# Two column blocks resized to 376, the first block in units of four chunks, the second by banks with the turns between the next step's matmuls

## The chip, the core and the metric

The kernel runs on one core of a Trainium2 chip. Its engines work side by side and meet through semaphores: PE multiplies matrices into PSUM, ACT and DVE read PSUM and write SBUF, POOL issues the loads of the input and computes a little, SP issues the stores of the output. The metric is the device time of one execution in microseconds; lower is better.

## What is computed

The input `x` is 8 x 3008 x 256. A Fourier transform over the sequence and over the width is taken, of it the real part, and each of its 24064 rows goes through a feed-forward layer of 2048 hidden units with a squared relu:

```python
X = np.fft.fft(np.fft.fft(x, axis=1), axis=2).real      # 8 x 3008 x 256
h = np.maximum(X.reshape(24064, 256) @ w_in, 0.0)       # 24064 x 2048
out = (h * h) @ w_out                                    # 24064 x 256
```

## The kernel before

**The columns.** The transform along the sequence is made from tables of sines and cosines and from folded input, so that a *unit* (batch, even or odd frequencies) gives PE matmuls with results in a PSUM tile `pz` (`z_steps`, matmuls at L565). Of each unit one half of the columns is copied from PSUM by ACT (L576, or L583 where it was put off), the other half is made by DVE as twice an earlier partial sum `es` less the result (L594). They land in two SBUF rows of columns, `zc` (cosine part) and `zs` (sine part). All columns stand in one sequence, units one behind the other: unit (0,0) holds columns 0 to 751, unit (1,0) 752 to 1503, its first 376 copied and its last 376 made by DVE, unit (0,1) begins at 1504. The sequence is cut into *blocks* (`wins`): the first few by `FIRST` (L58), the rest of 512.

**A block.** For a block of `wn` columns the hidden layer has 16 *chunks* of 128 units; a *step* `s` takes two chunks. `gh` holds the transformed first weight in three rows of blocks: cosine, sine, and -2 times sine (the *turn*). A step is: `pq(s)`, four matmuls into a PSUM tile `ph` of two banks, one chunk to a bank (cosine L793, sine L794); `relu(s, 0)`, by ACT into `h2` columns 0 to `wn`; `turn(s)`, two matmuls (L816) that add the turn row to the same PSUM tile, which makes of each column the hidden values of the mirrored frequency; `relu(s, 1)`, by ACT, reversed, into columns `wn` to 2 `wn`; and later `power(s)`, DVE's square of `h2` (L833). The PSUM pool for `ph` has two tiles (`ps_h`, `bufs=2`), as have `ps_o` and `ps_z`.

**What lies between.** The order is written out by hand, engine by engine. Behind `pq(s)` and `relu(s, 0)` stands `others(s)`: the step's share of the *second product* of the block before (`ffn2_steps`: groups of 128 output rows, two jobs of eight matmuls a group at L678, a copy of the result by ACT at L693 and stores by SP), folds of the next batch's input on DVE, table steps, and, from step `lo` on, the z matmuls of the units that the next block needs. A block of `wn` columns gives the next block 2 `wn`/128 groups, rounded up: eight groups (16 jobs of eight) for 512, four (8 jobs) for 240.

**Block 0** (240 columns) is taken two steps at a time: two `pq`, two relus, the others, two turns, two relus. Its `others` make the later parts of `gh`: `gh_step(cc)` is four matmuls for 512 hidden units (L511), and `gh_scale` brings them to SBUF, by DVE (L501) or ACT (L499); `gh_turn` makes the turn row (L518). `gh_step(1)` is called ahead of the block, into one tile of `ps_h`, and scaled by one DVE operation. `z0(0,2)` and `z0(1,2)` are the copies and the DVE half of the columns that block 0 left over. `gh_nyq` (16 small matmuls, L526, and a DVE copy) makes `g2n`, which is first read in block 4.

**Block 1** (512 columns) has one job of the second product in a step, and its first relu is two ACT operations, one to a bank (L825). Its `others` fold batch 1: the fold ends in `od`, which `nyq` (L438, `py`) and the z matmuls of steps 6 and 7 read. Block 4 takes in its steps 4 and 6 another way, in which DVE does the second relu (`cosines` L802, `twice` L806, `sines` L811, L827).

Of the kernel before, what the change touches and what calls it, by code (L numbers as in the profile page):

```python
# [29 lines left out]
def kernel(  # L30
# [24 lines left out]
    NFC = F // P  # L55
    WN = 512

    FIRST = [240, 512, 512, 240, 512, 448]  # L58
    R23 = float(2.0 ** 23)

    RQ = (1, 3, 5, 0, 2, 4)
# [441 lines left out]
    def gh_step(cc, act=None):  # L503

        f0 = cc * 512
        fw = f0 % (F // 2)
        pg = ps_h.tile([P, 2, 512], F32, name="pg", tag="psh") if act is None else None
        for i, t in enumerate((c_all, s_n)):
            pt = ps_o.tile([P, 512], F32, name="pg", tag="po") if pg is None else pg[:, i, :]
            for c in range(2):  # L510
                nc.tensor.matmul(pt, t[:, c, 0:P], w16[f0 // (F // 2)][:, c, fw : fw + 512], start=(c == 0), stop=(c == 1))  # L511
            if pg is None:
                gh_scale(gh[:, i, f0 : f0 + 512], pt, act)
        return pg

    def gh_turn(cc):
        f0 = cc * 512
        nc.vector.tensor_scalar(out=gh[:, 2, f0 : f0 + 512], in0=gh[:, 1, f0 : f0 + 512], scalar1=turn2[:, 0:1], scalar2=None, op0=ALU.mult)  # L518
# [116 lines left out]
    run(*z0(0, 1))  # L635
    run(*z0(1, 0))
    run(*z0(1, 1))
    gh_pg = gh_step(1)
    gh_scale(gh[:, 0:2, 512:1024], gh_pg, False)
    gh_turn(0)  # L640
    gh_turn(1)

# [99 lines left out]
    for w in range(NW):  # L742
        g0, wn = wins[w]
        h2 = h2p.tile([P, NFC, 2 * WN], F16, name="h2", tag="h2")
        zcw, zsw = zwin(w)

        lo, hi = 0, NST - 2
        at = [[] for _ in range(NST)]
        post = [[] for _ in range(NST)]
        if w == 0:  # L750
            at[0] = [lambda: gh_step(2, True), lambda: gh_turn(2), f0s["v_even"]]
            at[2] = [lambda: gh_step(3, False), lambda: gh_turn(3)]
            rm = z0(0, 2) + z0(1, 2)
            at[4] = rm[0::2]
            at[5] = rm[1::2]
        elif w == 1:
            fj = fold_jobs(1)
            at = [[], fj[0:1], fj[1:2], fj[2:3], fj[3:5], [], [], []]
            post[5] = fj[5:6]
            lo, hi = 6, NST  # L760
        elif w == 2:
            te = table_steps(1)
            at = [[folds[1]["even"]], [lambda: te["freq"](), lambda: te["args"](0)], [lambda: f0s["v_part"](0)], [lambda: f0s["v_part"](1), f0s["even"], f0s["back"]],
                  [lambda: te["turns"](0)], [lambda: te["mods"](0)], [lambda: te["absm"](0), lambda: te["sins"](0)], [lambda: te["coss"](0)]]
        elif w == 3:
            at[0] = [lambda: te["weigh"]()]
            for st in range(4):
                at[1 + st // 2] = at[1 + st // 2] + f0s["late"][st : st + 1]
            at[3] = [folds[1]["back"]]
            lo, hi = 4, NST  # L770
        elif w in fold_at:
            fj = fold_jobs(fold_at[w])
            at = [[f] for f in fj[0:4]] + [[], fj[4:5], fj[6:7], fj[7:8]]
            post[6] = fj[5:6]
        elif w == win_of(col_of[1, 1]) - 1:
            for st in range(4):
                at[1 + st] = folds[1]["late"][st : st + 1]
            lo, hi = 5, NST
        if w in late_at:
            for st in range(4):  # L780
                at[(2, 4, 6, 7)[st]] += folds[late_at[w]]["late"][st : st + 1]
        zj, zl = [], []
        for u in need[w + 1]:
            zu = z_steps(u)
            zj += [(zu, 1, 0), (zu, 0, 0), (zu, 1, 1), (zu, 0, 1)]
        f2 = ffn2_steps(*old) if old else []
        phs = {}

        def pq(s):
            ph = phs[s] = ps_h.tile([P, 2, 512], F32, name="ph", tag="psh")  # L790
            for a in range(2):
                f0 = (2 * s + a) * P
                nc.tensor.matmul(ph[:, a, 0:wn], gh[:, 0, f0 : f0 + P], zcw[:, 0:wn], start=True, stop=False)  # L793
                nc.tensor.matmul(ph[:, a, 0:wn], gh[:, 1, f0 : f0 + P], zsw[:, 0:wn], start=False, stop=True)  # L794

        t2s = {}

        def cosines(s):
            ph = phs[s] = ps_h.tile([P, 2, 512], F32, name="ph", tag="psh")
            for a in range(2):  # L800
                f0 = (2 * s + a) * P
                nc.tensor.matmul(ph[:, a, 0:wn], gh[:, 0, f0 : f0 + P], zcw[:, 0:wn], start=True, stop=True)  # L802

        def twice(s):
            t2 = t2s[s] = tmp.tile([P, 3 * NE], F32, name="t2", tag="tt")[:, 0 : 2 * WN].rearrange("p (a n) -> p a n", a=2)
            nc.vector.scalar_tensor_tensor(out=t2[:, :, 0:wn], in0=phs[s][:, :, 0:wn], scalar=-2.0, in1=n2s[w, s][:, :, 0:wn], op0=ALU.mult, op1=ALU.add)  # L806

        def sines(s):
            for a in range(2):
                f0 = (2 * s + a) * P  # L810
                nc.tensor.matmul(phs[s][:, a, 0:wn], gh[:, 1, f0 : f0 + P], zsw[:, 0:wn], start=False, stop=True, skip_group_check=True)  # L811

        def turn(s):
            for a in range(2):
                f0 = (2 * s + a) * P
                nc.tensor.matmul(phs[s][:, a, 0:wn], gh[:, 2, f0 : f0 + P], zsw[:, 0:wn], start=False, stop=True, skip_group_check=True)  # L816

        def relu(s, sg):
            h = h2[:, 2 * s : 2 * s + 2, sg * wn : (sg + 1) * wn]
            if sg:  # L820
                h = rev_dim(h, 2)
            if w == 1 and not sg:

                for a in range(2):
                    nc.scalar.activation(h[:, a], phs[s][:, a, 0:wn], AF.Relu, bias=0.0, scale=-1.0)  # L825
            elif sg and s in t2s:
                nc.vector._custom_dve(TENSOR_ADD_SAT, out=h, in0=t2s[s][:, :, 0:wn], in1=phs[s][:, :, 0:wn], s0=BIG, s1=0.0)  # L827
            else:
                nc.scalar.activation(h, phs[s][:, :, 0:wn], AF.Relu, bias=0.0, scale=-1.0)  # L829

        def power(s, a, b):
            h = h2[:, 2 * s : 2 * s + 2, a * wn : b * wn]
            nc.vector.tensor_tensor(h, h, h, op=ALU.mult)  # L833

        def others(s):
            for j in at[s]:
                j()
            for j in spread(f2, s, NST):
                j()
            for j in post[s]:  # L840
                j()
            if s == lo:
                zl[:] = [j for zu, part, h in zj for j in zu(part, h)]
            if s >= lo:
                for j in spread(zl, s - lo, hi - lo) if s < hi else []:
                    j()

        def nyq(s):
            if w + 1 in diff and hi < NST - 1:
                if s == hi:  # L850
                    spread_nyq(w + 1)
                    nyq_rows(w + 1, diff[w + 1][0:1])
                elif s == hi + 1:
                    nyq_rows(w + 1, diff[w + 1][1:])
            if s == 0 and w in diff and w not in zns:
                spread_nyq(w)
                nyq_rows(w, diff[w])

        kept = []

        def settle():
            for k in kept:
                power(*k)
            kept.clear()
            let_go()

        ng = 2 if w == 0 else 1
        for s0 in range(0, NST, ng):
            ss = range(s0, s0 + ng)
            held["on"] = s0 + ng in diff.get(w, ())  # L870
            if s0 in diff.get(w, ()):
                cosines(s0)
                twice(s0)
                settle()
                others(s0)
                sines(s0)
                relu(s0, 0)
                relu(s0, 1)
                kept.append((s0, 0, 2))
                nyq(s0)  # L880
                continue
            for s in ss:
                pq(s)
            settle()
            for s in ss:
                relu(s, 0)
                if s == NST - 1:
                    power(s, 0, 1)
            for s in ss:
                others(s)  # L890
            nyq(s0)
            for s in ss:
                turn(s)
            for s in ss:
                relu(s, 1)
                kept.append((s, int(s == NST - 1), 2))
        held["on"] = False
        settle()
        if w == 0:
            gh_nyq()  # L900
        old = (w, h2)
    for j in ffn2_steps(*old, tail=True):
        j()
# [30 lines left out]
```

## Time and profile before

| what | value |
|---|---|
| three runs | 625.13, 625.15, 625.33 us; median 625.15 |
| profiled execution | 625.18 us, span in the trace 623.40 us |
| granted TensorE clock, mean | 0.998 |
| DVE, ACT busy | 74%, 68% of the span |
| first matmul of blocks 0, 1, 2, 3, 4 | 21.33, 33.04, 56.21, 80.54, 102.23 us |

The span runs from the first to the last recorded instruction; some 1.8 us of the time lie around it. A row of a time line gives start, length, engine, source line, what is written and read with its shape, how many in a row, and in brackets how long the engine was idle and what released it. Ends of matmuls are modelled, so the distance from start to start is the better measure of PE. Lengths of neighbours on ACT and DVE overlap by about 0.1 us, so there too the next start counts.

### The profile page before, as it was taken

To read this page: it belongs to the slowest core of one execution; us is meant where nothing else is said; L and a number is where in the kernel's file an instruction comes from. 1 tells how busy PE (TensorE), PEld (TensorE's weight loads), DVE (VectorE), ACT (ScalarE), POOL (GpSimd) and SP (SyncE) were. 2 spreads that over 40 slices of the span, in tenths; PEclk is the share of its full clock that TensorE was granted. 3 is DMA by queue.
4 is the path that set the end of the run, shared out by engine and by line. 5 is a ranking of instruction groups with operands and counts; after the bars stand their busy time and mean duration, and the time that the engine had idled before them with its cause. 6 is when DMAs were issued, how large, how long until landed. Compare 5 with 4: busy or idle time off the path is not lost.

```text
span 623.4 us, 11238 instructions
## 1 busy us (share of the span) xinstructions
PE 599.6 (96%) x4487; PEld 431.3 (69%) x4487; DVE 464.3 (74%) x567; ACT 423.3 (68%) x589; POOL 257.1 (41%) x202
## 2 busy tenths in 40 slices
PE   4789998899999999999999999999999999999997
PEld 2456686577677777777777777776777777777786
DVE  7686753886978869768788679876797787876761
ACT  6677766767767666776677675776667767666652
POOL 8302322356452292255422942347610446426310
PEclk9999999999999999999999999999999999999999
DMA  8746331136111731541116411173111221211112
GB/s 151 106 99 142 103 95 35 33 68 163 49 46 34 150 99 50 109 124 49 52 46 121 119 47 43 44 143 102 50 29 62 68 79 34 51 44 37 53 54 68
DMA packets 36539, 47.51 MB, mean 76 GB/s; under 512 B 4231, under 2 KB 30343, under 8 KB 36487
## 3 DMA queue, kind: packets, MB, share of 16 engines
q0 software_dynamic: 9344, 22.14, 17.8%
q1 hardware_dynamic: 26915, 24.44, 13.1%
q8 instruction: 35, 0.57, 0.4%
q10 hardware_dynamic: 228, 0.21, 0.1%
q14 instruction: 17, 0.14, 0.1%
HBM read 33.63 MB, written 27.84 MB: 99 GB/s over the span
## 4 chain that ended last, share of the span: by engine, by line
PE 86%; ACT 5%; DVE 3%; POOL 3%; DMA 1%; issue 1%; POOLq 0%; DVEq 0%
PE po L678 49%; PE ph L816 9%; PE ph L793 9%; PE ph L794 9%; PE pz L565 3%; PE ph L811 3%; PE ph L802 3%; ACT h L829 3%; DMA scr<-ev 1%; ACT h L825 1%; DVE t L806 1%; PE pn L730 1%; POOL n L739 1%; DVE h L833 1%; PE pg L511 0%
## 5 line engine op out<-in xcount | busy, mean ns | idle before, releaser
L829 ACT ACTIVATE h<-ph 128x1024 f16<-128x1024 f32 (+3 forms) x342 | 317.3, 968 | 83.4 <-PE ph L816 39.7
L678 PE MATMUL po<-wout,h 128*128 128x256 f16 (+1 forms) x3024 | 361.6, 273 | 0.0
L678 PEld LDWEIGHTS <-h 128*128 128x128 f16 (+1 forms) x3024 | 296.5, 98 | 71.6
L833 DVE TENSOR_TENSOR h<-h 128x2048 f16<-128x2048 f16 (+7 forms) x225 | 235.4, 1057 | 80.8 <-ACT h L829 78.8
L739 POOL TENSOR_SCALAR n<-zn,g2n 128x512 f32<-128x512 f16 (+2 forms) x100 | 179.5, 1810 | 169.4 <-ACT zn L731 169.0
L793 PE MATMUL ph<-zc,gh 128*128 128x512 f16 (+3 forms) x300 | 108.0, 363 | 5.4 <-DVE zc L594 2.2
L794 PE MATMUL ph<-zs,gh 128*128 128x512 f16 (+3 forms) x300 | 108.0, 363 | 0.0
L693 ACT ACTIVATE osb<-po 128x512 f32<-128x512 f32 (+2 forms) x94 | 54.9, 587 | 64.3 <-PE po L678 50.8
L816 PE MATMUL ph<-zs,gh 128*128 128x512 f16 (+3 forms) x300 | 84.2, 363 | 3.4 <-ACT h L825 1.9
L806 DVE SCALAR_TENSOR_TENSOR t<-ph,n 128x1024 f32<-128x1024 f32 (+2 forms) x50 | 60.1, 1203 | 33.3 <-PE ph L802 30.2
L827 DVE CUSTOM_DVE_ANT_0 h<-t,ph 128x1024 f16<-128x1024 f32 x46 | 56.1, 1220 | 16.6 <-ACT h L829 15.3
L794 PEld LDWEIGHTS <-gh 128*128 128x128 f16 x300 | 29.3, 98 | 37.4 <-issue 6.7
L793 PEld LDWEIGHTS <-gh 128*128 128x128 f16 x300 | 29.2, 98 | 31.0 <-DVE h L827 0.2
L816 PEld LDWEIGHTS <-gh 128*128 128x128 f16 x300 | 27.5, 97 | 12.2 <-issue 6.0
L447 POOL DMA_DIRECT2D scr<-ev x8 | 4.8, 596 | 65.9 <-DVE od L440 49.2
L811 PE MATMUL ph<-zs,gh 128*128 128x512 f16 (+2 forms) x100 | 29.3, 374 | 1.6 <-DVE t L806 1.6
L802 PE MATMUL ph<-zc,gh 128*128 128x512 f16 (+2 forms) x100 | 29.3, 375 | 0.0
L127 POOL DMA_DIRECT2D xo<-in_x_dram x8 | 6.3, 782 | 52.9 <-DVE fo L422 42.4
L570 ACT ACTIVATE es<-pz 128x376 f32<-128x376 f32 (+1 forms) x32 | 15.3, 483 | 13.8 <-PE pz L565 13.7
L132 POOL DMA_INDIRECT xo<-in_x_dram,idx_r x15 | 21.1, 1407 | 4.5 <-issue 4.3
L457 POOL DMA_INDIRECT rb<-scr,idx_r x16 | 19.8, 1237 | 4.9 <-issue 4.9
L802 PEld LDWEIGHTS <-gh 128*128 128x128 f16 x100 | 9.8, 98 | 11.4
(134 smaller groups left out, 338.5 us busy)
## 6 DMA issues: line engine op xcount, KB each, us to landing
out_dram<-osb SPq DMA_DIRECT2D x77, 128.0 KB
xo<-in_x_dram POOLq DMA_DIRECT2D x7, 768.0 KB, 6.7
scr<-ev POOLq DMA_DIRECT2D x8, 390.0 KB, 3.7
rb<-scr POOLq DMA_DIRECT2D x16, 130.0 KB
out_dram<-osb SPq DMA_DIRECT2D x12, 94.0 KB
w<-in_moe_w_in_dram POOLq DMA_DIRECT2D x2, 512.0 KB
wout<-in_moe_w_out_dram POOLq DMA_DIRECT2D x1, 1024.0 KB
out_dram<-osb SPq DMA_DIRECT2D x8, 75.0 KB
```

What stands on the lines that cost most here:

```text
L678: nc.tensor.matmul(po[0:m, j * D : (j + 1) * D], h2[:, fc, q : q + m], wout16[:, fc, :], start=(fc == 0), stop=(fc == NFC - 1))
L693: nc.scalar.activation(osb[0:mm].rearrange("p s d -> p (s d)")[:, lo:hi], po[0:mm, lo:hi], AF.Copy, bias=0.0, scale=HS * HS)
L739: nc.gpsimd.tensor_scalar(out=n2[:, a, 0:wn1], in0=zns[wt][:, 0:wn1], scalar1=g2n[:, fc : fc + 1], scalar2=None, op0=ALU.mult)
L793: nc.tensor.matmul(ph[:, a, 0:wn], gh[:, 0, f0 : f0 + P], zcw[:, 0:wn], start=True, stop=False)
L794: nc.tensor.matmul(ph[:, a, 0:wn], gh[:, 1, f0 : f0 + P], zsw[:, 0:wn], start=False, stop=True)
L802: nc.tensor.matmul(ph[:, a, 0:wn], gh[:, 0, f0 : f0 + P], zcw[:, 0:wn], start=True, stop=True)
L806: nc.vector.scalar_tensor_tensor(out=t2[:, :, 0:wn], in0=phs[s][:, :, 0:wn], scalar=-2.0, in1=n2s[w, s][:, :, 0:wn], op0=ALU.mult, op1=ALU ...
L811: nc.tensor.matmul(phs[s][:, a, 0:wn], gh[:, 1, f0 : f0 + P], zsw[:, 0:wn], start=False, stop=True, skip_group_check=True)
L816: nc.tensor.matmul(phs[s][:, a, 0:wn], gh[:, 2, f0 : f0 + P], zsw[:, 0:wn], start=False, stop=True, skip_group_check=True)
L827: nc.vector._custom_dve(TENSOR_ADD_SAT, out=h, in0=t2s[s][:, :, 0:wn], in1=phs[s][:, :, 0:wn], s0=BIG, s1=0.0)
L829: nc.scalar.activation(h, phs[s][:, :, 0:wn], AF.Relu, bias=0.0, scale=-1.0)
L833: nc.vector.tensor_tensor(h, h, h, op=ALU.mult)
```

## The change

`FIRST` becomes 240, 512, 376, 376, 512, 448: blocks 2 and 3, before of 512 and 240 columns, get 376 each; block 2 is then exactly the copied half of unit (1,0), block 3 its DVE half. All other blocks keep their columns.

Block 0 is written out in *quads*: four chunks in one PSUM tile, two to a bank (`quad`, eight matmuls), one relu of 960 values for the four, four turns, one relu, one power. `gh_step(1)` goes into two tiles of `ps_o`, scaled by two DVE operations, and `gh_nyq` moves to the end of block 1.

Block 1 is written by halves of a tile: `half(s, a)` is two matmuls into bank `a` and the relu of that bank; the two turns of a step stand between the halves of the next step, and the second product behind both. Blocks from 2 on keep their loop.

```diff
-    FIRST = [240, 512, 512, 240, 512, 448]
+    FIRST = [240, 512, 376, 376, 512, 448]
...
-    gh_pg = gh_step(1)
-    gh_scale(gh[:, 0:2, 512:1024], gh_pg, False)
+    gh_step(1, False)
...
-        if w == 0:
-            at[0] = [lambda: gh_step(2, True), lambda: gh_turn(2), f0s["v_even"]]
-            at[2] = [lambda: gh_step(3, False), lambda: gh_turn(3)]
-            rm = z0(0, 2) + z0(1, 2)
-            at[4] = rm[0::2]
-            at[5] = rm[1::2]
...
-            if w == 1 and not sg:
-
-                for a in range(2):
-                    nc.scalar.activation(h[:, a], phs[s][:, a, 0:wn], AF.Relu, bias=0.0, scale=-1.0)
...
+        def quad(p):
+            ph = phs[p] = ps_h.tile([P, 2, 512], F32, name="ph", tag="psh")
+            for c in range(4):
+                f0 = (4 * p + c) * P
+                o = ph[:, c // 2, (c % 2) * wn : (c % 2 + 1) * wn]
+                nc.tensor.matmul(o, gh[:, 0, f0 : f0 + P], zcw[:, 0:wn], start=(c % 2 == 0), stop=False, skip_group_check=True)
+                nc.tensor.matmul(o, gh[:, 1, f0 : f0 + P], zsw[:, 0:wn], start=False, stop=True, skip_group_check=True)
...
+        def half(s, a):
+            if a == 0:
+                phs[s] = ps_h.tile([P, 2, 512], F32, name="ph", tag="psh")
+            f0 = (2 * s + a) * P
+            nc.tensor.matmul(phs[s][:, a, 0:wn], gh[:, 0, f0 : f0 + P], zcw[:, 0:wn], start=True, stop=False)
+            nc.tensor.matmul(phs[s][:, a, 0:wn], gh[:, 1, f0 : f0 + P], zsw[:, 0:wn], start=False, stop=True)
+            nc.scalar.activation(h2[:, 2 * s + a, 0:wn], phs[s][:, a, 0:wn], AF.Relu, bias=0.0, scale=-1.0)
+
+        def half_turn(s, a):
+            f0 = (2 * s + a) * P
+            nc.tensor.matmul(phs[s][:, a, 0:wn], gh[:, 2, f0 : f0 + P], zsw[:, 0:wn], start=False, stop=True, skip_group_check=True)
+
+        if w == 0:
+            rm = z0(0, 2) + z0(1, 2)
+            run(lambda: quad(0), lambda: quad_relu(0, 0), lambda: quad(1), lambda: quad_relu(1, 0), f0s["v_even"])
+            run(lambda: quad_turn(0), lambda: quad_relu(0, 1), lambda: gh_step(2, True), lambda: gh_turn(2))
+            run(lambda: quad_power(0), lambda: quad_turn(1), lambda: quad_relu(1, 1), *rm[0::2])
+            run(lambda: quad(2), lambda: quad_relu(2, 0), lambda: gh_step(3, False), lambda: gh_turn(3), lambda: quad_power(1))
+            run(lambda: quad(3), lambda: quad_relu(3, 0), *rm[1::2])
+            run(lambda: quad_turn(2), lambda: quad_relu(2, 1), lambda: quad_power(2), lambda: quad_turn(3), lambda: quad_relu(3, 1), lambda: quad_power(3))
+        elif w == 1:
+            half(0, 0)
+            half(0, 1)
+            for s in range(NST):
+                half_turn(s, 0)
+                if s + 1 < NST:
+                    half(s + 1, 0)
+                half_turn(s, 1)
+                relu(s, 1)
+                if s + 1 < NST:
+                    half(s + 1, 1)
                 settle()
-                others(s0)
-                sines(s0)
-                relu(s0, 0)
...
+                if s == NST - 1:
+                    power(s, 0, 1)
+                others(s)
+                kept.append((s, int(s == NST - 1), 2))
+            gh_nyq()
...
-        if w == 0:
-            gh_nyq()
         old = (w, h2)
```

`settle()` emits the powers that were kept back from the step before; `kept` holds them.

More of the change, by code (lines that the diff above doesn't have):

```diff
@@ L749 @@
         post = [[] for _ in range(NST)]
-        if w == 0:
-            at[0] = [lambda: gh_step(2, True), lambda: gh_turn(2), f0s["v_even"]]
-            at[2] = [lambda: gh_step(3, False), lambda: gh_turn(3)]
-            rm = z0(0, 2) + z0(1, 2)
-            at[4] = rm[0::2]
-            at[5] = rm[1::2]
-        elif w == 1:
+        if w == 1:
             fj = fold_jobs(1)
@@ L821, in relu @@
                 h = rev_dim(h, 2)
-            if w == 1 and not sg:
-                for a in range(2):
-                    nc.scalar.activation(h[:, a], phs[s][:, a, 0:wn], AF.Relu, bias=0.0, scale=-1.0)
-            elif sg and s in t2s:
+            if sg and s in t2s:
                 nc.vector._custom_dve(TENSOR_ADD_SAT, out=h, in0=t2s[s][:, :, 0:wn], in1=phs[s][:, :, 0:wn], s0=BIG, s1=0.0)
@@ L865, in settle @@
             let_go()
[L867 to L873, printed above, removed]
-                settle()
-                others(s0)
-                sines(s0)
-                relu(s0, 0)
[L878 to L886, printed above, removed]
+        def quad(p):
[5 more added lines that the diff above has]
+                nc.tensor.matmul(o, gh[:, 1, f0 : f0 + P], zsw[:, 0:wn], start=False, stop=True, skip_group_check=True)
@@ new lines, in quad_turn, with quad_relu @@
+        def quad_turn(p):
+            for c in range(4):
+                f0 = (4 * p + c) * P
+                o = phs[p][:, c // 2, (c % 2) * wn : (c % 2 + 1) * wn]
+                nc.tensor.matmul(o, gh[:, 2, f0 : f0 + P], zsw[:, 0:wn], start=False, stop=True, skip_group_check=True)
+        def quad_relu(p, sg):
+            h = h2[:, 4 * p : 4 * p + 4, sg * wn : (sg + 1) * wn]
+            if sg:
+                h = rev_dim(h, 2)
+            nc.scalar.activation(h.rearrange("p (b c) n -> p b c n", b=2), phs[p][:, :, 0 : 2 * wn].rearrange("p b (c n) -> p b c n", c=2), AF.Relu, bias=0.0, scale=-1.0)
@@ new lines, in quad_power @@
+        def quad_power(p):
+            h = h2[:, 4 * p : 4 * p + 4, 0 : 2 * wn]
+            nc.vector.tensor_tensor(h, h, h, op=ALU.mult)
+        def half(s, a):
[5 more added lines that the diff above has]
+            nc.scalar.activation(h2[:, 2 * s + a, 0:wn], phs[s][:, a, 0:wn], AF.Relu, bias=0.0, scale=-1.0)
@@ L887 @@
                 if s == NST - 1:
                     power(s, 0, 1)
-            for s in ss:
                 others(s)
[L891 to L894, printed above, removed]
-                relu(s, 1)
-                kept.append((s, int(s == NST - 1), 2))
+                kept.append((s, int(s == NST - 1), 2))
+            gh_nyq()
+        for s in range(NST) if w > 1 else ():
+            held["on"] = s + 1 in diff.get(w, ())
+            if s in diff.get(w, ()):
+                cosines(s)
+                twice(s)
+                settle()
+                others(s)
+                sines(s)
+                relu(s, 0)
+                relu(s, 1)
+                kept.append((s, 0, 2))
+                nyq(s)
+                continue
+            pq(s)
+            settle()
+            relu(s, 0)
+            if s == NST - 1:
+                power(s, 0, 1)
+            others(s)
+            nyq(s)
+            turn(s)
+            relu(s, 1)
+            kept.append((s, int(s == NST - 1), 2))
```

## The prediction, on record before the changed kernel ran

> **What bounds the kernel now.** I read the page, then a table by stage, PE's waits, and the time lines of PE and ACT for the stages that the change touches. The first row of the page:
>
> ```profile
> PE 599.6 (96%) x4487; PEld 431.3 (69%) x4487; DVE 464.3 (74%) x567; ACT 423.3 (68%) x589; POOL 257.1 (41%) x202
> ```
>
> PE is the bound, so only its gaps can move the end. The table by stage, cut at the first matmul of each of blocks 0 to 4, says where they lie (stretch, length, then busy time of PE, PEld, DVE, ACT, POOL, then granted clock):
>
> ```profile
> 21.33:33.04 11.71, 8.49 (x73) 5.82 (x72) 9.75 (x17) 9.11 (x20) 3.22 (x3) 1.00 0.49 77
> 33.04:56.21 23.17, 20.56 (x133) 12.41 (x129) 17.64 (x26) 18.68 (x32) 4.06 (x3) 1.00 0.63 123
> 56.21:80.54 24.33, 24.33 (x177) 17.22 (x176) 17.04 (x25) 18.07 (x22) 5.49 (x9) 1.00 0.28 92
> 80.54:102.23 21.69, 20.23 (x198) 18.38 (x196) 9.93 (x26) 13.05 (x26) 3.45 (x4) 1.00 0.28 80
> 102.23:124.00 21.77, 19.37 (x131) 12.26 (x131) 15.79 (x21) 16.28 (x24) 9.12 (x4) 1.00 0.07 24
> 124.00:623.40 499.40, 494.25 (x3728) 359.01 (x3726) 379.18 (x425) 335.20 (x445) 216.85 (x144) 1.00 0.28 72
> ```
>
> Blocks 0, 1, 3 and 4 hold 3.2, 2.6, 1.5 and 2.4 us of idle PE; the 499 us behind them, whose code is the same in both kernels, hold 5.2. PE's waits name the releasers (total, times, longest):
>
> ```profile
> PE ph L793 <- DVE zc L594: 2.2, 2, 1.5
> PE ph L816 <- ACT h L825: 1.9, 6, 0.4
> PE ph L793 <- ACT h L829: 1.7, 3, 0.8
> ```
>
> One step of block 1, on PE and then on ACT (start, length):
>
> ```profile
> 33.69 0.38 PE L794 MATMUL ph<-zs,gh 128*128 128x512 f16 x1
> 33.90 1.04 PE L678 MATMUL po<-wout,h 128*128 128x256 f16 x8
> 35.24 0.59 PE L816 MATMUL ph<-zs,gh 128*128 128x512 f16 x2 [0.30 <-ACT h L825]
> 35.67 0.38 PE L793 MATMUL ph<-zc,gh 128*128 128x512 f16 x1
> ```
>
> ```profile
> 34.10 1.08 ACT L825 ACTIVATE h<-ph 128x512 f16<-128x512 f32 x2 [0.69 <-PE ph L794]
> 35.87 1.02 ACT L829 ACTIVATE h<-ph 128x1024 f16<-128x1024 f32 x1 [0.68 <-PE ph L816]
> 36.79 1.08 ACT L825 ACTIVATE h<-ph 128x512 f16<-128x512 f32 x2
> ```
>
> A step is a loop PE, ACT, PE: turn, relu of the mirror half, two relus of the next tile, turn. It takes 0.63 + 0.92 + 1.08 + 0.05 = 2.68 us (35.24 to 37.92); PE's own work in it is 2.16. About 0.5 us a step is to be won.
>
> **Prices, all from rows of before.** Matmul to matmul: 0.103 at 240 columns, 0.158 at 376 (L565, three in 0.475), 0.2155 at 512; eight of the second product 0.87. From the start of the last matmul to the ACT that waits for it: 0.30 at 240 columns (21.64 to 21.94), 0.41 at 512 (33.69 to 34.10), about 0.34 at 376. ACT's relu, length and start to next start: 512 wide 0.60 and 0.48, 1024 wide 1.02 and 0.92, 480 wide 0.575 and 0.47, 752 wide 0.78 (L285) and 0.69. End of a relu to the matmul that waits: 0.055. Not in the trace: a relu 960 wide over two banks. Two of 480 in a row take 1.05, which is the upper bound; the line between 480 and 1024 gives 0.965, which I take (start to start 0.865); 0.91 is the lower bound, the line's value at 896.
>
> **PE's own work does not change.** The block widths add up to 2016 columns before and after, and the groups of the second product to 32. Blocks 2 and 3 swap 512 and 240 columns for 376 each; four of the sixteen eights of block 3 move into block 4.
>
> **Block 0.** From PE's order and the waits that stand in the built program. The gh scaling of step 1 becomes two DVE operations (21.09 and about 21.75, ending 22.39). Units 0 and 1 of four chunks: PE at 21.33 and 22.16, the second held at its first sine until 22.44; ACT 22.35 and 23.36. Turn of unit 0 at 23.37, relu 24.23; gh scaling on ACT at 25.09 and 25.58; turn of unit 1 and its relu at 26.07, ending 27.03. Unit 2 waits for the scaled sines (26.17): PE ends its turnless part at 26.9, relu 27.26. Step 3 of gh runs on PE at 26.95, but its scaling on DVE comes behind a power of 1.07 us and is done at 28.9 (28.24 for the cosines). So unit 3 is held on PE until 28.96 at its first sine, and ACT idles to 29.87. Its relu, then the mirror relus of units 2 and 3, follow back to back: 29.87, 30.74, 31.60. Block 1's first matmul needs the tile that the relu of 30.74 frees: 31.70 + 0.055 = 31.76, against 33.04: **-1.28**. 0.4 of it is the g2n row of 16 matmuls, which comes back at the end of block 1. With the relu's bounds (four of eight lie on this path): -0.95 to -1.5. DVE's fold work, moved earlier with the load of the next x, lies beside this; its next reader is in step 5 of block 1.
>
> **Block 1.** The text puts each turn between the matmuls of the next step and gives each bank its own relu. What the program waits for is another matter: its tile of two banks is tracked as one. Before already shows it: the first L825 needs only bank 0, whose sine matmul, started at 33.26 with length 0.38, was done at 33.64, and it starts at 34.10, after the fourth matmul. In the changed program's listing with waits, the first matmul of the second half carries a wait on ACT, which by its count is the relu of the first half; and the turn of a step waits for the relu of the *second* half. So, from a turn at t: first half of the next step on PE at t + 0.215, its second matmul at t + 0.43, relu at t + 0.84; the mirror relu 0.48 later; the second half's relu 0.92 later, 0.60 long; the turn 0.055 after it. **0.84 + 0.48 + 0.92 + 0.60 + 0.055 = 2.895 us a step, where before has 2.68.** PE stalls 0.63 between the halves and 0.1 ahead of the turn.
>
> [...] The row above, 34.10 and not 33.64, shows that this program waits by tile.
>
> At the start the first half is at 31.76, its relu at 32.47, the second half not before 33.12 (PE idle 0.9), its relu 33.75, the first turn at 34.40 (before 35.24). Six steps of 2.895 bring turn 6 to 51.77; before has it at 51.76, with one eight and a group of z matmuls (0.87 + 0.95) already done that still stand behind it now. Then: rest of step 6 to 55.51 (0.43 + 0.86 + 0.63 held + 0.87 + 0.95); step 7: turn 0.43, eight 0.87, z 0.95, g2n 0.4, to 58.17. The last copies of z on ACT: outputs at 57.06 (0.53 for two), sines 57.59, cosines 57.97 to 58.49. Block 2 starts at 58.54, before 56.21: block 1 alone **+3.6**, running sum **+2.33**. What goes: the 0.9 that block 2's first matmul waited for DVE L594, since block 2 is now only copied columns. What is late next is that ACT copy (0.38). DVE's fold chain ends near 49 and the py matmul asks at 51.7: hidden.
>
> **Blocks 2 to 4.** Block 2: 8 x (6 x 0.158 + 1.747) = 21.58, ends 80.12; ACT needs some 1.6 of each 2.7 us. Block 3: work 8 x 0.948 + 12 x 0.873 + 1.18 (z) = 19.24, where before has 20.07. Steps with one eight no longer cover the relu loop: 0.4 in step 0 (behind the cosine table and an output on ACT), 0.2 in step 2, 0.1 in step 6. The tail, from the last eight to block 4, goes through osb, two copies and four L594 as before: 2.13, plus 0.03 for the split output. Block 4 starts at 101.61, before 102.23. Block 4 gets 3.49 of work; its steps 1, 3, 5 and 7 now hold two eights and cover the loop: of before's 3.3 stalled, 2.0 remain (0.46 step 2, 0.67 and 0.15 the two DVE steps, 0.72 end). It ends at 125.34, before 123.80. So blocks 2 and 3 give **+0.54** beyond their work and block 4 **-1.33**. The tables and rb loads for block 4's z land some 2 us ahead of DVE (estimate from v's end, 69.9, plus the 12.2 to rb's landing that before needs).
>
> **Sum:** -1.28 + 3.62 + 0.54 - 1.33 = +1.55. The profiled execution took 625.18 (span 623.40 and 1.78 around it), the median shown is 625.15. Forecast **626.7**. The start of block 1 gives +-0.3, latencies of 0.05 in seven steps +-0.5, blocks 3 and 4 +-0.5: its own range is 625.7 to 627.8.
>
> **Rivals.** (1) The halves run freely by bank, and the end is on the other side. Then a step is ACT's 0.48 + 0.92 + 0.48 = 1.88 against PE's 2.16: 2.19 or so; the first turn is at 33.1 and DVE's fold (11.3 from the first power, 36.92 to 48.23 in before) is the bound at py, near 46.8; block 2 starts at 53.1, 5.4 earlier: 621.3. It decides wherever the first matmul of a second half follows its first half without a gap. For it: ACT is only 81% busy in this stage. Against: the wait in the listing, and 34.10. 0.10.
> (2) The loop costs what it did, 2.68 a step, because ACT's relu of one bank overlaps more than 0.48 suggests or the wait after it is shorter; then 6.5 x 0.21 less: 625.3, no change. For: the gap to win is 0.2 of a long chain. Against: each term is a row. 0.18.
> (3) Block 0 gains nothing: a relu waits for eight matmuls instead of four and unit 3 waits for DVE. Price 1.28: 628.0. For: ACT's idle of 1.7 ahead of unit 3 is new. Against: the chain above holds it already. 0.12.
> Forecast 0.60.
>
> **Chances.** This kernel's measurement can tell 0.2%, 1.25 us, from no change, so slower begins at 626.4, close under the forecast. The forecast gives 0.43 slower and 0.17 same; rival 1 faster; rival 2 0.13 same, 0.02 faster, 0.03 slower; rival 3 slower. Faster 0.12, same 0.30, slower 0.58. Range 624.6 to 628.4, which leaves out rival 1 and the outer ends of (2) and (3).
>
> **What would show it.** Right: first matmul of block 1 near 31.8, gaps of some 0.6 on PE between the halves put down to the relu of one bank, turns 2.9 apart, block 2 at 58.5, block 4 at 101.6. Wrong: turns 2.2 apart (rival 1) or 2.7 (2); block 1 starting at 33 (3); a stall in block 3's step 4 on rb; a block past 124 that shifts by more than the 1.5 us it is handed.

## The result, and the profile after

The changed kernel took **628.3 us** (median of eleven executions, 627.26 to 629.62) against 625.16 before; the ratio is 1.0047, 95% interval 1.0035 to 1.0058. The forecast was 626.7, its range 624.6 to 628.4. The execution that was profiled took 627.66 us, span 625.9. The eleven times lie in three groups, near 627.4, 628.4 and 629.6; why is the subject of half of the experiments below.

The first row of the page (busy time, share and instructions of each engine) hardly moves:

```profile
PE 601.1 (96%) x4487; PEld 431.6 (69%) x4487; DVE 464.0 (74%) x561; ACT 422.8 (68%) x582; POOL 257.3 (41%) x202
```

PE has the same 4487 matmuls; its busy time grows by 1.5 because ends are modelled (a lone matmul counts 0.38, one in a row 0.2155). The table by stage, cut at the first matmul of blocks 0 to 5, has the columns of the one before (stretch, length, busy time of PE, PEld, DVE, ACT, POOL, granted clock, then DMA):

```profile
21.32:31.74 10.42, 7.99 (x57) 5.21 (x56) 8.26 (x14) 7.75 (x12) 3.00 (x3) 1.00 0.68 112
31.74:58.50 26.76, 21.83 (x143) 12.82 (x143) 18.26 (x21) 19.73 (x32) 4.14 (x3) 1.00 0.48 95
58.50:80.11 21.61, 21.61 (x177) 17.21 (x176) 15.31 (x27) 14.27 (x21) 4.91 (x9) 1.00 0.33 107
80.11:101.76 21.65, 19.89 (x167) 15.51 (x164) 11.73 (x25) 16.09 (x26) 3.48 (x4) 1.00 0.25 70
101.76:125.45 23.69, 22.16 (x161) 15.20 (x161) 16.69 (x22) 16.73 (x25) 9.54 (x4) 1.00 0.09 28
125.45:625.90 500.45, 494.44 (x3728) 359.16 (x3727) 378.57 (x424) 335.40 (x446) 217.29 (x144) 1.00 0.28 72
```

Read the lengths: block 0 is 1.3 shorter (10.42 for 11.71), block 1 is 3.6 longer (26.76 for 23.17), and PE idles 4.9 of it. Beside the prediction:

| first matmul of | before | predicted | after |
|---|---|---|---|
| block 1 | 33.04 | 31.76 | 31.74 |
| block 1, first turn | 35.24 | 34.40 | 34.37 |
| block 1, turn of step 6 | 51.76 | 51.77 | 51.75 |
| block 2 | 56.21 | 58.54 | 58.50 |
| block 3 | 80.54 | 80.12 | 80.11 |
| block 4 | 102.23 | 101.61 | 101.76 |
| block 5 | 123.80 | 125.34 | 125.45 |

PE's waits (total, times, longest) name the new releaser, the relu of one bank (L886), in the first and the last of these lines:

```profile
PE ph L884 <- ACT h L886: 4.0, 8, 0.8
PE ph L804 <- DVE t L799: 1.5, 3, 0.6
...
PE ph L890 <- ACT h L886: 0.7, 1, 0.7
```

One step of block 1 on PE, then on ACT (start, length):

```profile
37.27 0.38 PE L890 MATMUL ph<-zs,gh 128*128 128x512 f16 x1
37.48 0.38 PE L884 MATMUL ph<-zc,gh 128*128 128x512 f16 x1
37.70 0.38 PE L885 MATMUL ph<-zs,gh 128*128 128x512 f16 x1
37.91 0.38 PE L890 MATMUL ph<-zs,gh 128*128 128x512 f16 x1
38.76 0.38 PE L884 MATMUL ph<-zc,gh 128*128 128x512 f16 x1 [0.47 <-ACT h L886]
38.98 0.38 PE L885 MATMUL ph<-zs,gh 128*128 128x512 f16 x1
39.19 1.03 PE L677 MATMUL po<-wout,h 128*128 128x256 f16 x8
40.16 0.38 PE L890 MATMUL ph<-zs,gh 128*128 128x512 f16 x1
```

```profile
38.11 0.60 ACT L886 ACTIVATE h<-ph 128x512 f16<-128x512 f32 x1 [0.90 <-PE ph L885]
38.61 1.02 ACT L818 ACTIVATE h<-ph 128x1024 f16<-128x1024 f32 x1
39.51 0.60 ACT L886 ACTIVATE h<-ph 128x512 f16<-128x512 f32 x1
```

From turn to turn 37.27 to 40.16, 2.89. The second turn starts at 37.91; the second half could follow at 38.13 and starts at 38.76, 0.05 after the relu of the *first* half (38.11 + 0.60). That relu reads the other bank. And ACT, which has 1.9 of work a step, idles 0.90 waiting for PE. So PE waits for ACT twice in a step (0.63 between the halves, and 0.1 ahead of the turn at 40.16, which starts 0.05 after the relu of the second half, 39.51 + 0.60), and ACT waits for PE once.

### The profile page after: what moved, and what is told of

Read it like the earlier page. It is cut to its first block, busy times and chain, and to the rows that moved or that the text cites. A ratio compares the mean times of both kernels' runs of the same rounds, so it can differ in the third digit from the quotient of the medians.

```text
span 625.9 us, 11226 instructions
## 1 busy us (share of the span) xinstructions
PE 601.1 (96%) x4487; PEld 431.6 (69%) x4487; DVE 464.0 (74%) x561; ACT 422.8 (68%) x582; POOL 257.3 (41%) x202
## 4 chain that ended last, share of the span: by engine, by line
PE 88%; ACT 4%; POOL 3%; DVE 2%; DMA 1%; issue 1%; POOLq 0%; DVEq 0%; ACTq 0%
PE po L677 50%; PE ph L809 8%; PE ph L786 8%; PE ph L787 8%; PE ph L804 3%; PE pz L565 3%; PE ph L795 3%; DMA scr<-ev 1%; DVE t L799 1%; ACT h L818 1%; ACT h L886 1%; ACT h L874 1%; PE ph L884 1%; PE pn L729 1%; POOL n L738 1%
## 5 line engine op out<-in xcount | busy, mean ns | idle before, releaser
L818 ACT ACTIVATE h<-ph 128x1024 f16<-128x1024 f32 (+3 forms) x326 | 308.8, 987 | 78.2 <-PE ph L804 38.6
L822 DVE TENSOR_TENSOR h<-h 128x2048 f16<-128x2048 f16 (+6 forms) x216 | 230.0, 1074 | 78.2 <-ACT h L818 76.4
L786 PE MATMUL ph<-zc,gh 128*128 128x512 f16 (+3 forms) x268 | 98.6, 368 | 2.3 <-DVE zc L594 1.4
L787 PE MATMUL ph<-zs,gh 128*128 128x512 f16 (+3 forms) x268 | 98.6, 368 | 0.0
L692 ACT ACTIVATE osb<-po 128x512 f32<-128x512 f32 (+3 forms) x95 | 54.9, 582 | 62.1 <-PE po L677 50.5
L799 DVE SCALAR_TENSOR_TENSOR t<-ph,n 128x1024 f32<-128x1024 f32 (+2 forms) x50 | 60.2, 1203 | 34.8 <-PE ph L795 30.1
L809 PE MATMUL ph<-zs,gh 128*128 128x512 f16 (+3 forms) x268 | 76.8, 368 | 0.7 <-ACT h L818 0.6
L787 PEld LDWEIGHTS <-gh 128*128 128x128 f16 x268 | 26.2, 98 | 31.4 <-issue 2.8
L786 PEld LDWEIGHTS <-gh 128*128 128x128 f16 x268 | 26.1, 98 | 28.8
L809 PEld LDWEIGHTS <-gh 128*128 128x128 f16 x268 | 24.4, 97 | 7.0 <-issue 1.7
L795 PEld LDWEIGHTS <-gh 128*128 128x128 f16 x100 | 9.8, 98 | 11.4
```

The lines of the kernel that those rows point to most:

```text
L692: nc.scalar.activation(osb[0:mm].rearrange("p s d -> p (s d)")[:, lo:hi], po[0:mm, lo:hi], AF.Copy, bias=0.0, scale=HS * HS)
```

## The experiments

All times are medians, with their range and number; ratios are against runs of the kernel before on the same chip, and are not quotients of the medians.

| kernel | time, us | ratio, 95% interval |
|---|---|---|
| sizes alone | 624.31 (624.18 to 626.36, 10) | 0.9990 (0.9981 to 0.9999) |
| quads alone | 623.86 (623.80 to 624.47, 10) | 0.9978 (0.9969 to 0.9987) |
| halves alone | 630.55 (629.12 to 633.40, 4) | 1.0072 (1.0054 to 1.0090) |
| sizes and quads, no halves | 623.23 (623.13 to 624.62, 7) | 0.9967 (0.9955 to 0.9978) |
| changed kernel again | 628.35 (627.90 to 630.41, 4) | 1.0042 (1.0025 to 1.0059) |
| changed kernel, third time | 627.38 (627.20 to 628.99, 5) | 1.0046 (1.0032 to 1.0060) |
| changed, gaps filled | 627.22 (627.18 to 627.32, 6) | 1.0032 (1.0020 to 1.0044) |
| the same again | 627.23 (627.15 to 627.30, 6) | 1.0032 (1.0020 to 1.0044) |
| changed, single-bank tiles | 622.00 (621.70 to 622.32, 4) | 0.9944 (0.9928 to 0.9961) |
| the same again | 621.91 (621.64 to 623.13, 5) | 0.9950 (0.9936 to 0.9964) |
| and six DVE operations | 621.63 (621.26 to 623.97, 6) | 0.9950 (0.9938 to 0.9962) |
| and eight matmuls early | **621.29** (621.25 to 621.31, 5) | 0.9935 (0.9922 to 0.9949) |

### Which part costs the time

No halves: the changed kernel, block 1 by the loop of before.

```diff
-        for s in range(NST) if w > 1 else ():
+        for s in range(NST) if w > 0 else ():
...
+            if w == 1 and not sg:
+                for a in range(2):
+                    nc.scalar.activation(h[:, a], phs[s][:, a, 0:wn], AF.Relu, bias=0.0, scale=-1.0)
```

> The change without its third part: sizes and quads as changed, block 1 with the loop of before (four matmuls, two relus of one bank, the second product, two turns, one relu), g2n at the end of block 1. Theory (the halves wait for a relu of the other bank, because the tile of two banks is tracked as one, and this alone makes the change slower): block 1 starts at 31.74 as in the changed kernel, turns are 2.68 apart again, block 2 starts near 54.8 (56.21 less 1.30 from block 0, plus 0.4 for g2n, less the 0.9 that block 2 waited for DVE, plus 0.38 for the copy by ACT) instead of 58.50, and the time is near 623.3 (622.8 to 624.0). Rival (the sizes of blocks 2 and 3 or something behind block 4 cost the time, the loop does not): still at or above 625, with block 5 later than 123.8.

Measured 623.23. Block 1 starts at 31.74, block 2 at 54.44 (0.36 earlier than expected, for a reason that sizes alone shows below), block 5 at 121.39. The turns, on PE:

```profile
33.94 0.59 PE L809 MATMUL ph<-zs,gh 128*128 128x512 f16 x2 [0.30 <-ACT h L817]
...
36.62 0.59 PE L809 MATMUL ph<-zs,gh 128*128 128x512 f16 x2 [0.35 <-ACT h L817]
```

They are 2.68 apart again. So the halves make block 1 longer by 26.76 - 22.70 = 4.06, and with them gone the change is a gain.

Halves alone: the kernel before with only block 1 by halves.

> The kernel before with the third part alone: block 1 by halves, sizes and block 0 as before. Theory (the loop of halves is 2.9 a step and costs 3.6 in block 1): turns 2.9 apart, block 2 starts near 59.8 (33.04 plus the 26.4 that block 1 took in the changed kernel without g2n, plus up to 0.9 for the half that DVE makes), time near 628.8 (628.2 to 629.4). Rival (the loop costs what it did, and the loss comes with the sizes): near 625.2.

Measured 630.55, the lowest 629.12. Slower, as the theory said, and by more. In the profiled execution (633.40) the turns behind 45 us are 2.90 apart (45.24, 48.14, 51.03), but it also holds two stretches at half clock, shown below; so this run gives the sign and the step, not the size.

Sizes alone (`FIRST` changed, nothing else) and quads alone (the kernel without halves, `FIRST` as before):

> The kernel before with the first part alone: blocks 2 and 3 of 376 columns. Worked out from the traces so far (22.30 of block 1 without g2n where block 2 waits no longer for DVE, 66.95 from block 2 to block 5): block 2 near 55.35, block 5 near 122.3 instead of 123.8, time near 623.8 (623.5 to 624.2). Rival (the sizes gain nothing by themselves, what was forecast for blocks 1 and 4 is given back): 625.2.

Measured 624.31, just above the range, with block 2 at 55.74 and block 5 at 122.69, both 0.4 later than expected. I had taken 0.4 for g2n off block 1's length; but block 1 is 22.69 long without g2n and 22.70 with it. Without it PE waits 0.25 for ACT's copy of z instead: at the end of block 1 the 16 small matmuls cost nothing.

> The kernel before with the second part alone: block 0 in quads, g2n at the end of block 1, block 1 and the sizes as before. Block 1 starts at 31.74, block 2 near 55.3 (56.21 less 1.30 plus 0.4 for g2n), block 5 near 122.9, time near 624.3 (624.0 to 624.8). Rival (what block 0 gains is eaten by the wait of block 2 for DVE's half of the columns): block 2 at 56.2, time 625.2.

Measured 623.86, a little under the range, with block 1 at 31.75, block 2 at 54.92 and block 5 at 122.52. Blocks 2 and 5 are 0.4 earlier than expected for the same reason: here g2n runs while block 2 waits for DVE's half, and 0.35 of that wait is still left behind it.

### Is it the tile, or the banks?

Each half gets a PSUM tile of its own, one bank wide: the pool of two-bank tiles is closed at block 1, one of four single banks opened, and the first opened again for block 2. The order of the matmuls is the changed kernel's. Two more things differ: the mirror relu is two operations, and the pools of `ph` are opened with `reuse_waits="tile"`, which the changed kernel does not set.

```diff
-            if a == 0:
-                phs[s] = ps_h.tile([P, 2, 512], F32, name="ph", tag="psh")
+            p1 = phs[s, a] = hp["p"].tile([P, 512], F32, name="p1", tag="ps1")
...
-                relu(s, 1)
+                half_mirror(s, 0)
+                half_mirror(s, 1)
```

> The changed kernel with one thing altered: in block 1 each half has a PSUM tile of its own, one bank wide, so that the program waits by bank; order of the matmuls unchanged, the mirror relu is two operations of 512 instead of one of 1024. Theory (the gap between the halves is the wait on the tile and nothing else): no gap between the halves, a step is bound by PE's 2.16 or ACT's four times 0.48, turns of one step to the next 2.2 apart, PE waits for DVE's fold at py near 47, block 2 starts near 53.1 and the time is near 622.0 (621.3 to 622.8). Rival (PE and ACT can't work on neighbouring banks side by side at full speed, or the mirror relu of two operations costs as much as the gap): turns 2.6 to 2.9 apart, matmuls or relus longer than 0.2155 and 0.48 from start to start, and 625.5 to 627.5.

Measured 622.00 and, run again, 621.91. One step on PE and its ACT:

```profile
35.47 0.38 PE L899 MATMUL p<-zs,gh 128*128 128x512 f16 x1
...
36.12 0.38 PE L899 MATMUL p<-zs,gh 128*128 128x512 f16 x1
36.34 0.38 PE L893 MATMUL p<-zc,gh 128*128 128x512 f16 x1
36.55 0.38 PE L894 MATMUL p<-zs,gh 128*128 128x512 f16 x1
36.77 1.04 PE L687 MATMUL po<-wout,h 128*128 128x256 f16 x8
37.64 0.38 PE L899 MATMUL p<-zs,gh 128*128 128x512 f16 x1
```

```profile
36.32 0.60 ACT L895 ACTIVATE h<-p 128x512 f16<-128x512 f32 x1 [0.24 <-PE p L894]
36.81 1.08 ACT L903 ACTIVATE h<-p 128x512 f16<-128x512 f32 x2
```

The second half (36.34) follows the turn at once, while ACT reads another bank from 36.32 on. Matmuls still start 0.215 apart and the relus 0.49, so the two don't slow each other. Steps alternate between 2.17 and 2.31 (turns 35.47, 37.64, 39.95); block 2 starts at 53.05. Block 1 takes 21.24 (31.81 to 53.05), where the loop of before takes 22.70 and the halves in two-bank tiles 26.76. From block 2 to block 5 the kernel takes 66.96, the changed one 66.95, so the other pools cost or gain nothing there. The gap was the wait on the tile: it is gone with tiles of one bank, and the relu it waited for still runs at the same time. So the gap of 0.63 was not needed.

### Why the times fall in groups

The changed kernel again, unaltered:

> The changed kernel once more, unaltered. Its eleven times lay in three groups, near 627.4, 628.4 and 629.6, whose mean granted clock was 0.998 to 1.000, 0.996 and 0.994 to 0.995, while nine of eleven of the kernel before lay within 0.3 of each other. Theory (the upper groups are stretches of lower granted clock, not another order of the work): each time above 627.7 comes with a mean clock of 0.996 or less, and a trace of such a run has a stretch with a clock below 1.00 ahead of the last matmul, with every landmark before it as it was. Rival (another wait in the blocks behind 5, as the 0.38 at 163 us): times differ at the same clock.

The profiled execution took 630.41, 2.75 over the first; 2.44 of it stand at the last matmul already. From 15 to 33.8 us the two traces agree to 0.02. The table by stretches of 3.4, of this execution (the number behind POOL's is the granted clock):

```profile
30.40:33.80 3.40, 1.75 (x8) 0.77 (x8) 2.92 (x4) 2.72 (x5) 0.00 (x0) 1.00 1.08 211
33.80:37.20 3.40, 2.56 (x6) 0.80 (x6) 0.34 (x3) 1.88 (x3) 0.00 (x0) 0.50 0.27 52
37.20:40.60 3.40, 3.40 (x13) 1.82 (x12) 3.16 (x4) 0.82 (x3) 0.00 (x0) 0.50 0.01 2
```

The clock is 0.50 for 6.8 us, and block 2 starts at 60.93 instead of 58.50. Ahead of it stands the head of block 1, where PE has only 8 matmuls in 3.4 us: four of 0.103 and four of 0.2155, 1.27 us of streaming. The first profiled execution had the same 8 there, and its clock was 1.00:

```profile
30.40:33.80 3.40, 1.75 (x8) 0.77 (x8) 2.92 (x4) 2.72 (x5) 0.00 (x0) 1.00 1.08 212
```

The execution profiled at the changed kernel's third time has them too (PE busy 1.75, x8), also at 1.00. So the sparse stretch does not decide alone. The kernel with the halves alone runs at half clock at the head of block 1 too, and at a second place:

```profile
12.75:16.15 3.40, 1.59 (x9) 0.87 (x9) 3.33 (x4) 2.99 (x5) 3.17 (x4) 0.99 1.09 171
16.15:19.50 3.35, 3.35 (x12) 1.43 (x10) 1.09 (x2) 1.17 (x3) 1.32 (x3) 0.50 1.34 196
33.15:36.55 3.40, 2.21 (x25) 1.17 (x24) 2.67 (x9) 2.46 (x6) 0.00 (x0) 1.00 1.10 217
36.55:40.00 3.45, 2.71 (x7) 0.85 (x7) 0.00 (x0) 1.92 (x3) 0.00 (x0) 0.50 0.60 119
40.00:43.40 3.40, 3.40 (x13) 1.72 (x12) 3.26 (x4) 0.83 (x3) 0.00 (x0) 0.50 0.01 2
```

Here the clock is 0.50 for 3.4 us from 16.1 on and for 6.8 us from 36.55 on; behind each the next 3.4 us have 1.00 (19.50:22.90 and 43.40:46.80). In the 3.4 us ahead of them PE had 9 matmuls (busy 1.59) and 25 (busy 2.21), 16 of the 25 of one column. Why equal work keeps its clock in one execution and loses it in the next was not shown.

The expectation failed in one point: of the four times, only 630.41 came with a clock of 0.996 or less. 628.67 missed that narrowly (0.997), but 628.02 and 627.90 came with 1.000 and 0.998. On that occasion the kernel before scattered too (626.56 at 0.999). Some tenths come behind the last matmul: in the traces that kept their clock it starts at 620.68 (twice) and, with the filled gaps of the next test, at 620.67 and 620.69, while what follows, the last copies and stores, takes 5.20, 4.89, 4.75 and 4.75. Whether that was so in the two executions here is not known; they were not traced.

The test adds work. Six matmuls of 512 columns, read by nobody, go into the two gaps at the head of block 1:

```diff
             half(0, 0)
+            fill(3)
             half(0, 1)
+            fill(3)
```

> The changed kernel with six matmuls of 512 columns added at the head of block 1, three in each of the two gaps between the first halves and the first turn (PE stood still there for 0.92 and 0.84; three take 0.65); their result goes to a PSUM tile that nobody reads. Theory (the upper groups of the changed kernel's times come from the clock: a stretch of about 3.4 us in which PE streams only some 1.3 us is followed by 3.4 or 6.8 us at half the clock, and with the halves the head of block 1 is such a stretch): work is added and the time falls; all or nearly all runs lie at 627.3 to 627.9, the median near 627.5 instead of 628.3, no trace shows a clock of 0.50 behind 30 us. Rival (the groups have another cause, or any gap counts): three groups as before, median 628.3 or, if the fillers are in the way, later.

Measured 627.22, six executions within 0.14, a little under the expected range. The head of block 1 is where it was (31.74, 33.09, 34.37), only the gaps are full:

```profile
32.17 0.81 PE L895 MATMUL pf<-zc,gh 128*128 128x512 f16 x3
33.09 0.38 PE L884 MATMUL ph<-zc,gh 128*128 128x512 f16 x1
```

The filled and the unfilled kernel had run on different occasions, so both were run again together on one chip:

> The changed kernel once more, beside the one with the six matmuls that fill its gaps, on one chip: the first two looks at it were made on other occasions than the look at the filled kernel. Theory (the head of block 1 halves the clock in a part of the executions): times spread from 627.2 to 629.6 or more, at least a third of them above 628. Rival (the spread belongs to the chip and the occasion): as narrow as the filled kernel beside it.

> The changed kernel with the six matmuls of 512 columns in the two gaps at the head of block 1, beside the unaltered one. Theory: all but one or two times at 627.1 to 627.5. Rival (the spread belongs to the chip and the occasion): the same spread as the unaltered kernel beside it.

Unfilled: 627.20, 627.27, 627.38, 628.97 and 628.99, the last two with a mean clock of 0.996 and 0.995; none reached the 629.6 that was expected. Filled: 627.15 to 627.30. The low ends are equal, the upper group is gone. Two of 5 against none of 6 would be little by itself. In all, 11 of 20 executions of the unfilled kernel lie above 628, ten of them with a mean clock of 0.997 or less, and none of 12 of the filled one.

### The late 0.38

Block 5 is 1.65 later than before, the work behind 163 us 2.04, which is 0.39 more (0.38 by the starts of the matmuls). The step is one product with the cosines on DVE (L806 before, L799 after), shown for before and after:

```profile
159.95 1.22 DVE L806 SCALAR_TENSOR_TENSOR t<-ph,n 128x1024 f32<-128x1024 f32 x1 [0.30 <-PE ph L802]
```

```profile
161.99 1.23 DVE L799 SCALAR_TENSOR_TENSOR t<-ph,n 128x1024 f32<-128x1024 f32 x1 [0.71 <-PE ph L795]
```

Its matmuls start at 159.25 and 160.90, so it waits 0.70 behind them in the one and 1.09 in the other, and PE behind it waits 0.58 instead of 0.19. The kernels without halves and with single-bank tiles show the same. They have six DVE instructions fewer than before. So six were put back into the single-bank kernel, in block 2, where DVE has time:

```diff
+            at[6] = at[6] + [lambda: nc.vector.memset(padt, 0.0)] * 6
```

> The kernel with single-bank tiles and six small DVE operations (one value per partition) added in step 6 of block 2, where DVE is idle half of the time. The kernels that hold the quads have six DVE instructions fewer than before, and in each of them the product with the cosines near 157 to 162 us starts 0.39 later behind its matmul than before does, so PE waits 0.57 instead of 0.19; a load of instructions stands right behind it. [...] Rival (the delay comes from the order of the loads or from POOL): the wait stays at 0.57, time 621.8 to 622.1.

With the six back, the forecast was a wait of 0.19 and a profiled execution near 621.4.

```profile
156.08 1.22 DVE L811 SCALAR_TENSOR_TENSOR t<-ph,n 128x1024 f32<-128x1024 f32 x1 [0.29 <-PE ph L807]
```

The wait is 0.19 again and the profiled execution takes 621.30 instead of 621.77; 0.39 of these 0.47 arise at this place, 0.08 ahead of it. Sizes alone (two DVE instructions fewer) and quads alone (four fewer) also wait 0.19. So in these runs the product was 0.39 late with six DVE instructions fewer ahead of it, and not with two or four fewer or with six put back. What makes it late was not shown. One packet of q14, which the page lists as an instruction queue, starts 0.68 behind the product's start in the changed kernel (162.67 for 161.99) and 5.2 ahead of it in the kernel before (154.79 for 159.95); whether it has a part in the delay was not shown either.

This kernel still had one time of 623.97, with a clock of 0.996, and two near 622 with 0.998. Last, the early place: in the set-up, where `idle(n)` issues matmuls whose only use is to keep PE busy, twelve for four.

```diff
     to["sins"](1)
-    idle(4)
+    idle(12)
```

> The single-bank kernel with the six small DVE operations, and in the set-up ahead of block 0 twelve of the matmuls that only keep PE busy where there were four (their result is not read), so that the stretch from 12 to 15 us, in which PE streams 1.4 of 3.4 us when the clock came up early, streams some 2.0. Theory (the times above the lowest group are half-clock stretches that follow such a stretch): all runs at 621.2 to 621.5, none near 622 or 624. Rival (the upper times have another cause): a spread as in the kernel without the twelve, 621.26 to 623.97.

> The single-bank kernel unaltered, beside the one with the six DVE operations and the twelve matmuls on the same chip. [...] Rival (the six operations gain nothing, the 0.47 between the two profiled executions was chance): lowest times within 0.1 of the other.

Without the six operations and the eight matmuls the forecast was a lowest time 0.4 higher, and some times above 622. Measured 621.25 to 621.31 in all five executions, beside 621.64 to 623.13 without the six operations and the eight matmuls. The six operations without the eight matmuls (621.26 to 623.97) ran on another chip, so that the eight matmuls took the upper times away is likely and not shown. This version beats both kernels: 3.9 us under the kernel before, 7.0 under the changed one.

## Why the prediction was right, and where it failed

- **Block 0, -1.28:** measured -1.30. The relu of 960 was the open price. ACT's row for the last three (three in 2.69) gives 0.86 from start to start, where the forecast took 0.865:

```profile
29.86 2.69 ACT L874 ACTIVATE h<-ph 128x960 f16<-128x960 f32 x3 [1.61 <-PE ph L862]
```

- **Block 1, 2.895 a step:** measured 2.90, from 34.37 to 51.75 in six steps. The sum held because each term was a row, and because the wait was read from the built program and not from the intent of the source.
- **Blocks 2 to 4, +0.54 and -1.33:** measured from the same marks (101.76 - 58.50 = 43.26 for 43.07 predicted; 23.69 for 23.73). With blocks 0 and 1 that is +1.65 at block 5, where +1.55 was forecast.
- **The step that failed** is the one that took everything behind block 5 as equal because its code is equal, and the clock as given. With six DVE instructions fewer ahead of it, equal code had one product start 0.39 later. That is the prediction's own last sign of being wrong, a block past 124 that shifts by more than it is handed. With the 0.39 the sum is 625.15 + 1.65 + 0.39 = 627.19, and the kernel with its gaps filled takes 627.22. The rest up to the median of 628.3, 1.1 us, is mostly the clock, since it is gone with the gaps filled: the prediction itself found PE idle 0.9 and more at the head of block 1, and priced that idle time only as time. The rows of before show 1.00 in every stage, so the price was not to be read there; that the stage became sparser was.
- **Luck:** the median of 628.3 lies 0.1 inside the upper end of the stated range and outside the sum's own 625.7 to 627.8, where 5 of the 11 times are. The range holds it by chance, because neither the 0.39 nor the clock was in it. Rival 3 was priced at 628.0, closest of all, and its mechanism, a block 0 that gains nothing, is wrong.
- **The rivals:** that the halves run by bank would have been right with single-bank tiles. The price worked out for it, block 2 at 53.1 and 621.3, came as 53.05 and, with DVE's late delay gone and the eight matmuls in the set-up, 621.29. The loop at 2.68 and a block 0 without gain are ruled out by the marks.

## What to carry to other kernels

Interleaving by bank gained here only where what the program waits on is one bank wide (block 1 took 21.24, and 26.76 with tiles of two banks): look at the waits of the built program, and where a tile spans two banks give each its own. Where a change thins out PE's stream as at the head of block 1 here (1.27 of 3.4 us, at 0.50 behind it in one of three profiled executions), look at the granted clock of several executions, not of one. Six matmuls that nobody reads, put into gaps that stand anyway, cost nothing here (lowest time 627.15, and 627.20 without them), and none of 12 executions with them lies above 628. Price a part alone before it goes in with others: here two parts gained 1.9 together, and the third lost 4.0; with tiles of one bank the same third part gains 1.2 (623.23 to 622.00).

## What the hardware showed that was not expected

- The granted clock was 0.50 for 6.8 us in one of three profiled executions of the changed kernel, behind 3.4 us in which PE streamed 1.27; in the other two it was 1.00 behind the same 8 matmuls. With the halves alone it was 0.50 for 3.4 and for 6.8 us. Through the 6.8 us PE was busy for 2.56 of the first 3.40 (2.71 of 3.45 with the halves alone) and for all of the second; behind them the clock was 1.00 (40.80:44.20 and 43.40:46.80). The 6.8 us cost 2.43 at block 2.
- ACT reading one PSUM bank while PE wrote another slowed neither in the single-bank kernel: 0.49 and 0.215 from start to start.
- Six DVE instructions of one value each, added some 85 us ahead, made one product wait 0.39 less for its start and the kernel 0.47 shorter in the profiled execution.
